# Own tiles for queries and keys, loads issued in four places of a batch, tail scores one batch ahead: attention with a routed expert layer behind it

## The chip, the cores and the metric

The kernel runs on one core of a Trainium2 chip. The metric is the device time of one execution in microseconds (us), taken as the median of several executions.

## The reference, cut to what matters

Eight batches of eight heads of retention attention (a causal product without a softmax, each head with its own decay), and then a mixture of eight experts of which each token takes one:

```python
# q, k, v: (8, 8, 576, 64); x: 4608 tokens of 512; w1: (8, 512, 1024); w2: (8, 1024, 512)
scores = scale * np.matmul(q, k.transpose(0, 1, 3, 2))
Dmat = np.where(rel >= 0, gamma[:, None, None] ** rel[None, :, :], 0.0)
ret = scores * Dmat[None, :, :, :]
attn_out = np.matmul(ret, v)
...
expert_idx = np.argmax(logits, axis=1)
h = np.maximum(x[mask] @ w1[e], 0.0)
out[mask] = gate_w[mask, None] * (h @ w2[e])
```

## The kernel before, in words

**Two stages.** The attention runs batch by batch over roughly the first quarter of the time; the experts follow. Within a manual schedule every engine, and the queue of SyncE (SP) on which nearly all transfers are issued, does its work in the order in which the program writes it. So a transfer that waits for its buffer holds up the transfers written behind it.

**One batch.** A batch has 576 positions: four chunks of 128 and a tail of 64. Heads go in pairs p = 0 to 3. `load_qk(b, p)` (L525) brings queries and keys of one pair into one tile `qkt` of two halves, by one transfer (two for batch 0); the pool has eight such tiles, two batches' worth. `load_k` (L537) brings the keys a second time in the other layout (`kt`, two buffers), `load_v` (L544) the values (`vt`, two buffers). `load_batch(b)` (L940) issues all six in a row: four `qkt`, then `kt`, then `vt`.

**The loop** (L1036) runs, for each batch b from 1, `scores(b)`, `tokens(b - 1)`, `products(b)`, and then `load_batch(b + 2)`:

- `scores(b)` (L979): for each pair `emit_A` (L710), the products of keys and queries inside the chunks (L716, TensorE), which VectorE multiplies by the decay (L725); behind each, `scale_q` (L704) on GpSimd. At its end `scale_k(b + 1)` (L683, GpSimd) on the next batch's `kt`.
- `tokens(b - 1)` (L989): the router's work for the batch before: logits (L905, L913), ranks, transposes of four or five tiles of tokens (L882) that ScalarE copies into `y` (L883) and SP stores to `xd` (L886).
- `products(b)` (L1005): `emit_U` (L733, L743: keys times values), `emit_O` (L791, L799: scores times values), `emit_At` (L831, L838: the scores of the tail, then the decay on VectorE into `pt`, L840), `emit_S` (L807, L815: the state times the queries) and `emit_Ot` (L845, L855: the tail's output, from `pt`).

`qkt` of batch b is read last by `emit_Ot(b)`, `kt` of batch b by `emit_U(b)`, `vt` of batch b by `emit_Ot(b)`; the loads of batch b + 2 take these buffers.

**PSUM banks.** There are eight. `Banks.tile` (L110) hands them out: in batch 0 from two rings of four, from batch 1 on from one ring of eight (`Banks.joint`, set at L1039), and behind the loop from a list of free banks (`Banks.loose`, L121), to which `done` (L125) returns one when the program has written its last use. Which buffer a matmul has to wait for follows from this order alone.

**Behind the loop** (L1047 on) come the last routing and the first expert's products, in an order written out by hand.

Of the kernel before, what the change touches and what calls it, by code (L numbers as in the profile page):

```python
# [95 lines left out]
def retention_moe(ctx: ExitStack, tc: tile.TileContext, qk, kn, v0s, vs, w1, w2, head, cst, out):  # L96
# [28 lines left out]
    def done(ps):  # L125

        if Banks.loose is not None:
            Banks.loose.append(ps)
# [375 lines left out]
    with ExitStack() as att:  # L504
# [2 lines left out]
        a2 = att.enter_context(tc.tile_pool(name="a2", bufs=2))  # L507
        a1 = att.enter_context(tc.tile_pool(name="a1", bufs=1))

        qkt, xT, xC = {}, {}, {}  # L510
        w0 = {}

        def w0_load(c):
# [8 lines left out]

        both = (nc.sync, nc.scalar)

        def load_qk(b, p):  # L525
            t = qkp.tile([P, 2, S], F32, name="qkt")
            if b == 0:
                for i, on in enumerate(both):
                    on.dma_start(out=t[:, i], in_=qk[b, p, i])
            else:  # L530
                nc.sync.dma_start(out=t, in_=qk[b, p].rearrange("i p s -> p i s"))
            qkt[b, p] = t

        kt, vt_ = {}, {}
        KW = NCH * DM
# [155 lines left out]
        def turn_k(p):  # L691

            ps = psa.tile([P, 512], F32, name="a")
            for c in range(NCH):
                nc.tensor.transpose(ps[:, c * P : (c + 1) * P], qkt[0, p][:, 1, c * P : (c + 1) * P], ident)
            g = cc("gneg").rearrange("p (c h) -> p c h", c=NCH)[:, :, 2 * p : 2 * p + 2]
            nc.vector.tensor_tensor(
                out=kview(0)[:, :, p * P : (p + 1) * P].rearrange("p c (h d) -> p c h d", h=2),
                in0=ps.rearrange("p (c h d) -> p c h d", c=NCH, h=2),
                in1=g.unsqueeze(3).broadcast_to([P, NCH, 2, D]),  # L700
                op=ALU.mult,
            )

        def scale_q(b, p):  # L704
            q = qkt[b, p][:, 0, P : NCH * P]
            nc.gpsimd.tensor_tensor(out=q, in0=q, in1=gsb[:, p, :], op=ALU.mult)  # L706

        Pm, Pt = {}, {}

        def emit_A(b, p):  # L710
            t = qkt[b, p]
            ps = [psa.tile([P, 512], F32, name="a") for _ in range(2)]
            for c in range(NCH):
                for h in range(2):
                    hs = slice(h * D, (h + 1) * D)
                    nc.tensor.matmul(  # L716
                        ps[h][:, c * P : (c + 1) * P],
                        t[hs, 1, c * P : (c + 1) * P],
                        t[hs, 0, c * P : (c + 1) * P],
                        start=True,  # L720
                        stop=True,
                    )
            pm = raws[(0, 1, 4, 5)[p]][:, :1024].rearrange("p (h c n) -> p h c n", h=2, c=NCH)
            for h in range(2):
                nc.vector.tensor_tensor(  # L725
                    out=pm[:, h],
                    in0=ps[h].rearrange("p (c n) -> p c n", c=NCH),
                    in1=decay[:, 2 * p + h].unsqueeze(1).broadcast_to([P, NCH, P]),
                    op=ALU.mult,
                )  # L730
            Pm[b, p] = pm

        def emit_U(b):  # L733
            k, v, T = kview(b), vview(b), Tst
            for c2 in range(NCH // 2):
                ps = psm.tile([P, 512], F32, name="m")
                u = ps.rearrange("p (c r d) -> p c r d", c=2, r=NP)
                for ci in range(2):
                    c = 2 * c2 + ci
                    for p in range(NP):  # L740
                        for h in range(2):
                            hd = 2 * p + h
                            nc.tensor.matmul(  # L743
                                u[h * D : (h + 1) * D, ci, p, :],
                                k[:, c, hd * D : (hd + 1) * D],
                                v[:, c, hd, :],
                                start=True,
                                stop=True,
                            )
                for ci in range(2):  # L750
                    c = 2 * c2 + ci
                    if c == 0:
                        nc.scalar.copy(T[:, 0], u[:, 0])
                    else:
                        nc.vector.tensor_tensor(out=T[:, c], in0=u[:, ci], in1=T[:, c - 1], op=ALU.add)

        def emit_U0(g):
            k, v, T = kview(0), vview(0), Tst
# [48 lines left out]
        def emit_S(b, g):  # L807

            T = Tst
            x, xc = x_tiles(b)  # L810
            for c in range(1, NCH):
                for p in (2 * g, 2 * g + 1):
                    for h in range(2):
                        hs = slice(h * D, (h + 1) * D)
                        nc.tensor.matmul(  # L815
                            Po[b, p][side(p, h), c * P : (c + 1) * P],
                            T[hs, c - 1, p, :],
                            qkt[b, p][hs, 0, c * P : (c + 1) * P],
                            start=False,
                            stop=(c == NCH - 1),  # L820
                        )
            for p in (2 * g, 2 * g + 1):
                po = Po.pop((b, p))
                if b % 2 == 0:
                    nc.scalar.copy(x[:, p, :], po)
                else:
                    copy = nc.vector.tensor_copy if (b, g) == (B - 1, 1) else nc.scalar.copy
                    copy(xc[:, p, D:], po[:, :D])
                    copy(x[:, p, : 512 - D], po[:, D:])

        def emit_At(b):  # L831
            ps = psa.tile([P, 512], F32, name="a")
            u = ps[:, : NP * TL].rearrange("p (r n) -> p r n", r=NP)
            for p in range(NP):
                for h in range(2):
                    hs = slice(h * D, (h + 1) * D)
                    t = qkt[b, p]
                    nc.tensor.matmul(u[hs, p, :], t[hs, 1, 512:], t[hs, 0, 512:], start=True, stop=True)  # L838
            pt = a2.tile([P, NP, TL], F32, name="pt")
            nc.vector.tensor_tensor(  # L840
                out=pt, in0=u, in1=cc("decayt").rearrange("p (r n) -> p r n", r=NP), op=ALU.mult
            )
            Pt[b] = pt

        def emit_Ot(b):  # L845
            vt, T, pt = vtview(b), Tst, Pt.pop(b)
            ps = [(psm if b else psa).tile([P, 512], F32, name="m") for _ in range(2)]
            u = [x[:, : NP // 2 * TL].rearrange("p (r n) -> p r n", r=NP // 2) for x in ps]
            for r in range(NP // 2):
                for last in (False, True):  # L850
                    for odd in range(2):
                        p = 2 * r + odd
                        for h in range(2):
                            hs = slice(h * D, (h + 1) * D)
                            nc.tensor.matmul(  # L855
                                u[odd][side(p, h), r, :],
                                T[hs, NCH - 1, p, :] if last else vt[hs, p, :],
                                qkt[b, p][hs, 0, 512:] if last else pt[hs, p, :],
                                start=(r == 0 and not last),
                                stop=(r == NP // 2 - 1 and last),  # L860
                            )
            x, xc = x_tiles(b)
            dst = xc[:, :, :TL] if b % 2 == 0 else x[:, :, 512 - D :]
            g = cc("gtail").rearrange("p (r n) -> p r n", r=NP)
            for odd in range(2):
                nc.vector.tensor_tensor(out=dst[:, odd::2], in0=u[odd], in1=g[:, odd::2], op=ALU.mult)


        def tile_src(b, g):
# [109 lines left out]
        def scores(b):  # L979
            for p in range(NP):  # L980
                emit_A(b, p)
                scale_q(b, p)
                if (b, p) == (B - 1, 0):
                    for i in range(3):
                        gather(0, i, BEG)
            if b + 1 < B:
                scale_k(b + 1)

        def tokens(b):  # L989
# [6 lines left out]
                route_onehot(b - 1)  # L996
            for g in range(group_tiles(b)[1]):
                route_tile(b, g)
            route_turn(b)
            if b == B - 2:  # L1000
                for i in range(2):
# [3 lines left out]
        def products(b):  # L1005
            end = b == B - 1
            emit_U(b)
            if end:
                xprep(0, 2)
                w0_load(2)  # L1010
# [7 lines left out]
            if end:  # L1018
                low = [w0_high(0), w0_high(1, nc.gpsimd)]
                w0_load(3)  # L1020
            emit_At(b)
            if end:
                for split in low:
                    split()
# [11 lines left out]
        for b in range(B):  # L1036
            if b == 0:
                first_batch()
                Banks.joint = every  # L1039
            else:  # L1040
                scores(b)
                tokens(b - 1)
                products(b)
            if b + 2 < B:
                load_batch(b + 2)
        loose_banks()
        b = B - 1  # L1047
        gates_power(slice(0, NT - 5))
        first = [mm1_in(PAIRS[0], 0)]
# [554 lines left out]
```

## Time and profile before

| what | value |
|---|---|
| median of 3 runs | 570.35 us (569.89 to 570.95) |
| the profiled execution's own time | 571.25 us |
| its span, first to last instruction | 569.3 us |
| mean granted TensorE clock | 1.000 |
| TensorE (PE) busy | 98% of the span |
| VectorE (DVE) / ScalarE (ACT) / GpSimd (POOL) busy | 73% / 67% / 42% |

In the rows PE is TensorE's matmul, PEld its weight load, and a name with q is the queue of that engine. L716 is line 716. A row of a group of instructions gives the busy time and the mean of one; a row of waits gives us in total, how many, and the longest. "issue" is time in which an engine waited for nothing that the profile shows. DMA share is the mean busy share of the 16 DMA engines.

### The profile page before, as it was taken

How to read it: one execution, taken by the hardware profiler on the slowest of the kernel's cores; microseconds unless marked ns; L12 is line 12 of the kernel's file. 1: busy time of each engine (PE TensorE's matmuls, PEld its weight loads, DVE VectorE, ACT ScalarE, POOL GpSimd, SP SyncE). 2: the span in 40 equal slices, each digit the busy share in tenths (PEclk: the TensorE clock that was granted, in tenths of full speed). 3: DMA queues.
4: the chain of work that ended last, by engine and by line, in shares of the span. 5: the costliest groups of instructions: out<-in, count | busy, mean ns of one | idle time of the engine just before them, and what ended most of it. 6: DMA issues, size and time to landing. Idle time of an engine off the chain costs nothing.

```text
span 569.3 us, 13412 instructions
## 1 busy us (share of the span) xinstructions
PE 556.9 (98%) x5258; PEld 510.1 (90%) x5258; DVE 417.3 (73%) x938; ACT 381.7 (67%) x696; POOL 236.6 (42%) x233
## 2 busy tenths in 40 slices
PE   9999998999999999999999999999999999999996
PEld 8888898999998899889989988998899899889986
DVE  4755778779876868877887888688778778786810
ACT  1246554447759887987787788779877877867611
POOL 6674345554456740562065126405620750242012
PEclk9999999999999999999999999999999999999999
DMA  9999999877469583557447445837574574422201
GB/s 319 390 395 340 350 335 378 307 269 266 167 207 184 174 201 119 148 161 185 122 145 206 129 117 186 186 111 168 163 150 131 156 200 133 133 101 84 75 38 49
DMA packets 81089, 109.24 MB, mean 192 GB/s; under 512 B 42328, under 2 KB 43772, under 8 KB 81024
## 3 DMA queue, kind: packets, MB, share of 16 engines
q1 hardware_dynamic: 71920, 86.24, 50.0%
q0 software_dynamic: 7696, 19.95, 10.7%
q10 hardware_dynamic: 1408, 2.17, 1.1%
q8 instruction: 42, 0.69, 0.5%
q14 instruction: 23, 0.19, 0.1%
HBM read 80.27 MB, written 19.94 MB: 176 GB/s over the span
## 4 chain that ended last, share of the span: by engine, by line
PE 78%; DMA 12%; issue 3%; DVE 3%; ACT 2%; POOL 1%; POOLq 0%; SPq 0%; ACTq 0%; DVEq 0%
PE m L1281 19%; PE a L1213 15%; PE m L1213 11%; PE a L1281 10%; DMA out<-y,sid 9%; PE a L716 3%; PE a L459 2%; PE a L799 2%; PE m L716 2%; PE m L459 2%; DMA xd<-y 2%; PE m L799 2%; PE a L882 1%; PE m L882 1%; PE m L743 1%
## 5 line engine op out<-in xcount | busy, mean ns | idle before, releaser
L1281 PE MATMUL m<-w2s,hs 128*128 128x512 f32 x600 | 138.8, 389 | 0.0
L1281 PEld LDWEIGHTS m<-w2s,hs 128*128 128x128 f32 x600 | 112.3, 188 | 22.9
L1257 POOL DMA_INDIRECT out<-y,sid x41 | 47.0, 1147 | 193.0 <-DVE wsum L1135 125.7
L1281 PE MATMUL a<-w2s,hs 128*128 128x512 f32 (+1 forms) x384 | 83.6, 376 | 0.0
L1281 PEld LDWEIGHTS a<-w2s,hs 128*128 128x128 f32 x384 | 68.9, 188 | 13.1
L1213 PE MATMUL a<-xsb,w0s 128*128 128x320 f32 x342 | 57.9, 309 | 0.0
L375 POOL DMA_INDIRECT gt<-gd,gid x40 | 44.7, 1118 | 18.4 <-issue 10.8
L1213 PEld LDWEIGHTS a<-xsb,w0s 128*128 128x128 f32 x342 | 52.1, 188 | 0.0
L1184 ACT ACTIVATE hs<-y 128x320 fp32r<-128x320 f32 x84 | 39.3, 474 | 17.8 <-DVE y L1225 16.7
L362 POOL DMA_INDIRECT raw<-xd,gid x40 | 42.7, 1069 | 19.3 <-DVE sid L352 7.6
L1177 DVE SCALAR_TENSOR_TENSOR hs<-y,hs 128x320 fp32r<-128x320 f32 x84 | 46.6, 568 | 2.0
L687 POOL TENSOR_TENSOR kt<-kt,cs 128x512 f32<-128x512 f32 x28 | 28.4, 1045 | 46.1 <-DMA kt<-kn 46.1
L410 ACT COPY raw<-raw 128x1024 uint16<-128x1024 uint16 x35 | 47.5, 1356 | 0.0
L445 ACT CAST xsb<-raw 128x128 fp32r<-128x128 f32 x70 | 32.1, 459 | 21.6 <-DVE raw L428 20.9
L1112 DVE TENSOR_TENSOR w2s<-raw,w2s 128x1024 fp32r<-128x1024 f32 x32 | 39.1, 1222 | 6.7 <-ACT w2s L1109 6.6
L1225 DVE TENSOR_TENSOR y<-a,y 128x320 f32<-128x320 f32 x47 | 22.7, 486 | 20.3 <-ACT y L1229 14.0
L403 ACT COPY raw<-raw 128x1024 uint16<-128x1024 uint16 x35 | 35.4, 1045 | 0.0
L1109 ACT CAST w2s<-raw 128x1024 fp32r<-128x1024 f32 x32 | 33.4, 1045 | 2.4 <-DMA raw<-w 2.4
L706 POOL TENSOR_TENSOR qkt<-qkt,gsb 128x384 f32<-128x384 f32 x32 | 31.3, 1006 | 7.2 <-DMA xd<-y 2.9
L1213 PE MATMUL m<-xsb,w0s 128*128 128x320 f32 x198 | 34.0, 309 | 0.0
L421 DVE TENSOR_TENSOR raw<-raw 128x256 f32<-128x256 f32 x35 | 14.8, 424 | 26.1 <-ACT raw L410 26.1
L1225 DVE TENSOR_TENSOR y<-m,y 128x320 f32<-128x320 f32 x37 | 18.1, 488 | 18.7 <-ACT y L1229 13.2
(258 smaller groups left out, 1198.5 us busy)
## 6 DMA issues: line engine op xcount, KB each, us to landing
raw<-w SPq DMA_DIRECT2D x64, 512.0 KB, 3.9
qkt<-qk SPq DMA_DIRECT2D x28, 576.0 KB, 7.9
xd<-y SPq DMA_DIRECT2D x36, 256.0 KB, 9.9
vt<-vs SPq DMA_DIRECT2D x7, 1152.0 KB, 13.1
kt<-kn SPq DMA_DIRECT2D x7, 1024.0 KB, 10.9
qkt<-qk ACTq DMA_DIRECT2D x4, 288.0 KB, 5.3
qkt<-qk SPq DMA_DIRECT2D x4, 288.0 KB, 5.4
out<-y,sid POOLq DMA_INDIRECT x41, 3.3
```

The source lines that it names most:

```text
L362: nc.gpsimd.indirect_dma_start(out=t[:, XO : XO + DM], out_offset=None, in_=xd[:rows, :], in_offset=bass.IndirectOffsetOnAxis(ap=gid[:, a ...
L375: nc.gpsimd.indirect_dma_start(out=g[:, i : i + 1], out_offset=None, in_=gd[:, :], in_offset=bass.IndirectOffsetOnAxis(ap=gid[:, a : a + 1 ...
L403: nc.scalar.copy(far.rearrange("p (h n) -> p h n", h=2), near.rearrange("p (n h) -> p h n", h=2))
L410: nc.scalar.copy(far.bitcast(U16).rearrange("p (n h) -> p h n", h=2), near.rearrange("p (h n) -> p h n", h=2))
L1109: nc.scalar.copy(hi, u)
L1112: nc.vector.tensor_tensor(out=lo, in0=u, in1=hi.bitcast(F32), op=ALU.subtract)
L1177: nc.vector.scalar_tensor_tensor(out=lo, in0=part(src), scalar=0.0, in1=hi.bitcast(F32), op0=ALU.max, op1=ALU.subtract)
L1184: nc.scalar.activation(hi, part(src), AF.Relu)
L1213: nc.tensor.matmul(ps[:, :HC], w[:, ws, ka, d * P : (d + 1) * P], xop(kx, xsp)[:, d, :], start=(n in (1, 2, 5) and d == 0 and k == 0), sto ...
L1225: nc.vector.tensor_tensor(out=out[:, :HC], in0=x[:, :HC], in1=out[:, :HC], op=ALU.add)
L1257: put = nc.gpsimd.indirect_dma_start(out=out.rearrange("t (k n) -> (t k) n", k=k), out_offset=bass.IndirectOffsetOnAxis(ap=rows, axis=0), ...
L1281: nc.tensor.matmul(ps[:, :step], hs[:, hsp, f, i * P : (i + 1) * P], w[:, ws, f, n : n + step], start=(j == 0 and k == 0), stop=(j == NF - ...
```

## The change

Queries and keys get a tile each, of half the size, so that the keys' buffer of batch b is free of queries. The loads of a later batch are issued in four places instead of one: the keys of pair p of batch b + 2 behind `emit_A(b, p)`, the values of batch b + 1 behind the token tiles of `tokens(b - 1)`, `kt` of batch b + 2 behind `emit_U(b)`, and the queries of batch b + 2 at the end, where all of them were. The tail's scores are computed one batch ahead: `products(b)` calls `emit_At(b + 1)` where it called `emit_At(b)`, batch 1's are computed at the end of its `scores`, and the last batch's `products` has none. Banks come from the free list from batch 1 on.

```diff
+        def load_q(b, p):
+            qt[b, p] = qkp.tile([P, S], F32, name="qt")
+            nc.sync.dma_start(out=qt[b, p], in_=qk[b, p, 0])
+
+        def load_kT(b, p, on=nc.sync):
+            kT[b, p] = qkp.tile([P, S], F32, name="kT")
+            on.dma_start(out=kT[b, p], in_=qk[b, p, 1])
+
         def load_qk(b, p):
-            t = qkp.tile([P, 2, S], F32, name="qkt")
-            if b == 0:
-                for i, on in enumerate(both):
-                    on.dma_start(out=t[:, i], in_=qk[b, p, i])
-            else:
-                nc.sync.dma_start(out=t, in_=qk[b, p].rearrange("i p s -> p i s"))
-            qkt[b, p] = t
+            load_q(b, p)
+            load_kT(b, p, nc.sync if b else nc.scalar)
...
         def emit_A(b, p):
-            t = qkt[b, p]
+            q, k = qt[b, p], kT[b, p]
...
+                done(ps[h])
...
         def scores(b):
             for p in range(NP):
                 emit_A(b, p)
+                if 0 < b < B - 2:
+                    load_kT(b + 2, p)
                 scale_q(b, p)
...
+            if b == 1:
+                emit_At(b)
             if b + 1 < B:
                 scale_k(b + 1)
...
             for g in range(group_tiles(b)[1]):
                 route_tile(b, g)
+            if b + 2 < B:
+                load_v(b + 2)
             route_turn(b)
...
             emit_U(b)
+            if b + 2 < B:
+                load_k(b + 2)
...
-            emit_At(b)
+            if not end:
+                emit_At(b + 1)
...
             if b == 0:
                 first_batch()
-                Banks.joint = every
+                loose_banks()
+                for p in range(NP):
+                    load_kT(b + 2, p)
+                load_k(b + 2)
             else:
                 scores(b)
                 tokens(b - 1)
                 products(b)
             if b + 2 < B:
-                load_batch(b + 2)
-        loose_banks()
+                for p in range(NP):
+                    load_q(b + 2, p)
         b = B - 1
```

The other hunks put `done(...)` behind the last use of each bank in `emit_U`, `emit_S`, `emit_At` and `emit_Ot`, and write `qt` or `kT` where `qkt` stood.

## Rows read from the trace of the kernel before

**Rows 1.** The page, part 1: TensorE's busy time and instructions.

```profile
PE 556.9 (98%) x5258; PEld 510.1 (90%) x5258; DVE 417.3 (73%) x938; ACT 381.7 (67%) x696; POOL 236.6 (42%) x233
```

**Rows 2.** Busy time by stretch: span, PE, PEld, DVE, ACT, POOL, clock, DMA share, GB/s.

```profile
20.00:40.00 20.00, 19.24 (x439) 18.04 (x440) 11.48 (x31) 8.87 (x24) 12.02 (x13) 1.00 1.05 390
80.00:100.00 20.00, 18.22 (x434) 17.25 (x434) 14.16 (x40) 10.87 (x28) 7.94 (x8) 1.00 1.04 381
160.00:180.00 20.00, 20.00 (x141) 18.89 (x141) 12.41 (x28) 14.56 (x26) 9.77 (x10) 1.00 0.93 210
```

**Rows 3.** TensorE's waits in the first 200 us: total us, times, longest.

```profile
PE a L716 <- DMA xd<-y: 1.8, 1, 1.8
PE m L855 <- issue: 1.5, 1, 1.5
...
PE m L595 <- PEq L1595: 0.7, 1, 0.7
...
PE a L799 <- issue: 0.2, 1, 0.2
```

**Rows 4.** TensorE's timeline, 15 to 150 us: start, us, instruction, idle before it.

```profile
21.19 0.49 PE L716 MATMUL a<-qkt 64*128 64x128 f32 x4
...
40.89 1.29 PE L716 MATMUL m<-qkt 64*128 64x128 f32 x18 [1.15 <-issue]
...
89.95 0.37 PE L716 MATMUL a<-qkt 64*128 64x128 f32 x1 [1.78 <-DMA xd<-y]
...
122.82 2.06 PE L716 MATMUL a<-qkt 64*128 64x128 f32 x32
```

**Rows 5.** Busy time and counts from 0 to five of the waits' starts, columns as above.

```profile
0.00:39.74 39.74, 38.49 (x727) 35.74 (x728) 23.33 (x67) 11.76 (x29) 26.57 (x37) 1.00 1.01 365
0.00:53.08 53.08, 50.69 (x981) 47.02 (x981) 31.29 (x90) 18.72 (x47) 33.73 (x45) 1.00 1.02 372
...
0.00:70.19 70.19, 66.97 (x1361) 62.22 (x1362) 43.55 (x123) 27.02 (x68) 39.87 (x51) 1.00 0.99 358
0.00:88.10 88.10, 83.37 (x1742) 77.72 (x1742) 57.04 (x156) 36.30 (x92) 49.32 (x60) 1.00 0.99 356
...
0.00:120.39 120.39, 113.38 (x2375) 105.88 (x2376) 80.29 (x227) 51.94 (x132) 63.76 (x75) 1.00 0.98 353
```

**Rows 6.** The page, part 3, the queue that carries instructions: packets, MB, share.

```profile
q8 instruction: 42, 0.69, 0.5%
```

**Rows 7.** Queues from 87.40 to 87.60 us.

```profile
q8 instruction: 1, 0.02, 31.9%
```

**Rows 8.** Queues from 89.95 to 94.55 us (no other queue has a row).

```profile
q1 hardware_dynamic: 756, 1.64, 101.1%
```

**Rows 9.** Queues from 89.95 to 94.70 us: the row that is new.

```profile
q8 instruction: 1, 0.02, 1.3%
```

**Rows 10.** Queues from 103.36 to 104.65 us.

```profile
q1 hardware_dynamic: 241, 0.43, 88.1%
q8 instruction: 1, 0.02, 6.1%
```

**Rows 11.** The page, part 6: transfers, count, KB each, median us to landing.

```profile
qkt<-qk SPq DMA_DIRECT2D x28, 576.0 KB, 7.9
xd<-y SPq DMA_DIRECT2D x36, 256.0 KB, 9.9
vt<-vs SPq DMA_DIRECT2D x7, 1152.0 KB, 13.1
kt<-kn SPq DMA_DIRECT2D x7, 1024.0 KB, 10.9
```

**Rows 12.** Busy time in four stretches of 4 us, columns as in the stretches above.

```profile
52.00:56.00 4.00, 3.38 (x106) 3.08 (x104) 2.73 (x9) 2.15 (x4) 2.04 (x3) 1.00 0.70 261
56.00:60.00 4.00, 4.00 (x93) 3.68 (x90) 3.84 (x7) 0.11 (x1) 3.69 (x4) 1.00 0.82 243
72.00:76.00 4.00, 4.00 (x84) 3.81 (x77) 3.99 (x9) 0.00 (x0) 3.43 (x4) 1.00 0.84 243
104.00:108.00 4.00, 4.00 (x121) 3.93 (x115) 3.60 (x11) 2.31 (x8) 2.70 (x3) 1.00 0.56 128
```

**Rows 13.** GpSimd's timeline: the keys' scaling waits for its load.

```profile
24.15 4.05 POOL L687 TENSOR_TENSOR kt<-kt,cs 128x512 f32<-128x512 f32 x4 [4.90 <-DMA kt<-kn]
...
35.89 4.08 POOL L687 TENSOR_TENSOR kt<-kt,cs 128x512 f32<-128x512 f32 x4 [3.83 <-DMA kt<-kn]
```

**Rows 14.** The chain that ended last: the tail's scores of batch 1.

```profile
34.33 0.61 PE m L838 x16
```

**Rows 15.** The queue of SP: issue of four loads, start and us.

```profile
36.69 3.18 SPq L531 DMA_DIRECT2D qkt<-qk  x4
```

More of the change, by code (lines that the diff above doesn't have):

```diff
@@ L508, in retention_moe @@
         a1 = att.enter_context(tc.tile_pool(name="a1", bufs=1))
-        qkt, xT, xC = {}, {}, {}
+        qt, kT, xT, xC = {}, {}, {}, {}
         w0 = {}
@@ L694, in turn_k @@
             for c in range(NCH):
-                nc.tensor.transpose(ps[:, c * P : (c + 1) * P], qkt[0, p][:, 1, c * P : (c + 1) * P], ident)
+                nc.tensor.transpose(ps[:, c * P : (c + 1) * P], kT[0, p][:, c * P : (c + 1) * P], ident)
             g = cc("gneg").rearrange("p (c h) -> p c h", c=NCH)[:, :, 2 * p : 2 * p + 2]
@@ L704, in scale_q @@
         def scale_q(b, p):
-            q = qkt[b, p][:, 0, P : NCH * P]
+            q = qt[b, p][:, P : NCH * P]
             nc.gpsimd.tensor_tensor(out=q, in0=q, in1=gsb[:, p, :], op=ALU.mult)
@@ L717, in emit_A @@
                         ps[h][:, c * P : (c + 1) * P],
-                        t[hs, 1, c * P : (c + 1) * P],
-                        t[hs, 0, c * P : (c + 1) * P],
+                        k[hs, c * P : (c + 1) * P],
+                        q[hs, c * P : (c + 1) * P],
                         start=True,
@@ L755, in emit_U @@
                         nc.vector.tensor_tensor(out=T[:, c], in0=u[:, ci], in1=T[:, c - 1], op=ALU.add)
+                done(ps)
         def emit_U0(g):
@@ L817, in emit_S @@
                             T[hs, c - 1, p, :],
-                            qkt[b, p][hs, 0, c * P : (c + 1) * P],
+                            qt[b, p][hs, c * P : (c + 1) * P],
                             start=False,
@@ L829, in emit_S @@
                     copy(x[:, p, : 512 - D], po[:, D:])
+                done(po)
         def emit_At(b):
@@ L836, in emit_At @@
                     hs = slice(h * D, (h + 1) * D)
-                    t = qkt[b, p]
-                    nc.tensor.matmul(u[hs, p, :], t[hs, 1, 512:], t[hs, 0, 512:], start=True, stop=True)
+                    nc.tensor.matmul(u[hs, p, :], kT[b, p][hs, 512:], qt[b, p][hs, 512:], start=True, stop=True)
             pt = a2.tile([P, NP, TL], F32, name="pt")
@@ L843, in emit_At @@
             Pt[b] = pt
+            done(ps)
         def emit_Ot(b):
@@ L857, in emit_Ot @@
                                 T[hs, NCH - 1, p, :] if last else vt[hs, p, :],
-                                qkt[b, p][hs, 0, 512:] if last else pt[hs, p, :],
+                                qt[b, p][hs, 512:] if last else pt[hs, p, :],
                                 start=(r == 0 and not last),
@@ L866, in emit_Ot @@
                 nc.vector.tensor_tensor(out=dst[:, odd::2], in0=u[odd], in1=g[:, odd::2], op=ALU.mult)
+                done(ps[odd])
         def tile_src(b, g):
```

## The prediction

> **What bounds the kernel now.** I began with the page's busy times: TensorE is busy 98% of the span [rows 1]. A load order can only win where it waits, so I went on to the busy time by stretch. There the experts' stage has no gap (20.00 of 20 us), while the attention loses 0.8 us of 20 at its start and 1.8 us at 80 to 100, and in those stretches the DMA engines are full, at 381 to 390 GB/s [rows 2]. TensorE's waits of the first 200 us come to eight lines, 7.4 us together, of which 0.7 are the start [rows 3]. So some 6.7 us, 1.2% of the time, is all that the waits shown could give back.
>
> None of these waits names a tile that the instruction reads or writes: most say "issue", and the longest is put down to a store of tokens. I counted what TensorE had done when they came. Matmuls and weight loads together stand at 1455, 1962, 2723, 3484 and 4751 [rows 5]; the differences are 507, 761, 761 and 1267, that is 2, 3, 3 and 5 times 253.5. The queue named "instruction" moved 42 packets of 16 KB [rows 6], and 10,516 matmuls and weight loads [rows 1] over 42 make 250 each. So TensorE waits at the ends of blocks of its own program. The wait before 89.95 us shows the course: a block came between 87.40 and 87.60 [rows 7], TensorE went on at 89.95 [rows 4], some 2.4 us behind it. The next packet came only 4.60 to 4.75 us later, with the load queue at 101% of 16 engines [rows 8, 9]. At 103.36, where that queue was running dry, it came within 1.3 us [rows 10]. So a block takes 4.65 + 2.4 = 7.0 us behind a full queue and 1.3 + 2.4 = 3.7 behind an empty one. A batch takes (122.82 - 21.19) / 6 = 16.9 us from batch 1 to 7 [rows 4], and a block (120.39 - 39.74) x 253.5 / (4751 - 1455) = 6.2 us [rows 5]. A full load queue therefore makes TensorE late, an empty one doesn't.
>
> The Trainium skill, "Runtime: NRT & Kernel Launch", section "Instruction fetch mechanics", says that instructions come in 16 KiB blocks of 256 and that the cost of crossing a boundary is "mostly hidden". By that rule the waits would have another cause and the change would leave them all. The block size agrees with the trace; "hidden" does not, behind a full queue.
>
> **The change part by part.** The sum is made against the profiled execution: 571.25 us, a span of 569.3 and 1.95 around it. That is 0.90 above the median of 570.35.
>
> *Bytes.* Nothing is saved: a batch loads 4 x 576 + 1152 + 1024 = 4480 KB and stores 4.5 x 256 KB [rows 11], 5.77 MB. At 388 GB/s that is 14.9 us of the 16.9 that a batch lasts. However the loads are spread, the queue has work for 88% of the time; spreading decides when, and how much lies in it.
>
> *When.* Keys (1.18 MB) are issued some 14 us earlier than now, `kt` (1.05 MB) some 7 us earlier, queries as now, values some 8 us later. On the whole the queue is given work earlier. The idle of the DMA engines, 30% of 52 to 56, 18% of 56 to 60 and 16% of 72 to 76 us [rows 12], 2.5 us together, gets filled; the other lull at 104 to 108 (44%) gets longer and starts sooner. So the first four batches have a full queue throughout, and the refills there stay as late as they are. What is won is won in batches 5 and 6: 2.5 us x 388 GB/s, nearly 1 MB, less in the queue. The waits that I find there are 1.78 us at 89.95 [rows 4], and about 0.5 each at 103 and 120, among the lines left out between the first and the last of the waits [rows 3]. I take half of these 2.8 us: **-1.4**. Ends: nothing (another block is late instead), and all 6.7 us of the waits shown if every block comes in time.
>
> *Tail scores one batch ahead.* This needs queries and keys of batch 2 while batch 1 is in its products. `kt` of batch 1 landed at 24.15 [rows 13]. Behind it on the queue now lie values of batch 1 (1.18 MB), then keys, `kt` and queries of batch 2 (1.18 + 1.05 + 1.18): 4.59 MB, 11.8 us, so the queries land at 36.0. The same sum for the old order (1.18 + 2.36 + 1.05) gives 36.0 for `kt` of batch 2; it landed at 35.89 [rows 13]. TensorE comes to these scores at 34.33, plus 0.5 for batch 1's that are now in front: 34.8 [rows 14]. It waits **+1.2 us**, and the state's and tail's products queue behind it. Further on it closes: values of batch 2 land at 36.0 + 3.41 MB / 388 = 44.8, some 1 us before they are needed, queries of batch 3 at 50.5, some 2 before. Ends: 0, if the refill that is late in this place anyway covers it, and 3 us, if the next two come late as well. The scores' own 0.6 us moves from batch 7 to batch 1: nothing.
>
> *Queue of SP.* Four more transfers a batch. Four cost 3.18 us of issue in a full queue [rows 15], of 16.9; nothing is issued late by it, since SP waits for buffers most of the time. Each new place stands behind work that TensorE has done by then. Cost 0; if SP were held up, the stores would be late, which only the routing reads.
>
> *Banks.* No wait of TensorE names a reader of a bank [rows 3]; a list in the order of release, with at most four banks of `emit_O` out, takes the place of a ring. Nothing, at most 0.5 us either way, by the shorter gaps behind the copies at a batch's end. `done` issues no instruction.
>
> *GpSimd and VectorE.* `kt` lands earlier, so GpSimd waits less than the 4.9 and 3.8 us of [rows 13]; TensorE isn't behind it, so nothing. The decay on the tail's scores has the same place on VectorE, and leaves batch 7: between 0 and -0.4.
>
> Sum: -1.4 + 1.2 - 0.2 = -0.4, 570.85 for the profiled execution, and 0.90 less for the median: **569.9 us**. That is no change: what a measurement here can tell is 0.2%, 1.14 us.
>
> **Rivals.**
>
> *The refills come in time (faster).* If a refill's wait goes by how much lies in the queue just then, and not by whether it has work, shorter bursts of at most some 2 MB, where 4.6 MB were issued at once, let most blocks of batches 3 to 7 through. Then the waits from 60 us on go (1.5, 1.8, 0.5, 0.5 and 0.2, 4.5 us), less 1.2 for the first: 570.35 - 3.3 = 567.0. For it: 1.3 us against 4.65 [rows 8 to 10]. Against it: 88% of the time has work to move. At its far end all 6.7 go and blocks that now come just in time gain too, down to 563. Half-size transfers for queries and keys would help the same way. The Trainium skill, "DMA: Bandwidth & Descriptors", section "Queues, rings and completion order", says that a DMA engine goes round its queues packet by packet; by that rule smaller transfers put less in front of a refill. No row here separates transfer sizes.
>
> *Data late in the first batches (slower).* The order puts keys that are needed 25 us later ahead of values and queries needed within 15. If the queries of batch 2 land 1 us later than my sum, at 37, the wait is 2.2; everything behind shifts little, as the queue is full, so the wait stays. If blocks 2 to 4 are late besides, by 0.5 each, no gain later: 570.35 + 3.0 = 573.3. It decides from the point where the queue at 24 us holds over 4.6 MB in front of these queries.
>
> *The waits have another cause, or stay as they are.* Only the 1.2 remain: 571.5; the smaller part of slower.
>
> **How the numbers follow.** Forecast, within 0.2% of the median: 0.38, since the bytes and their rate don't move and the two terms nearly cancel. Refills in time: 0.37, of which 0.07 are below 565.5. Slower: 0.25, two thirds of it at 571.5 to 573 and 0.07 beyond. The range leaves out 0.07 below and 0.07 to 0.1 above: 565.5 to 572.8. The likeliest case alone spans 569.2 to 571.5.
>
> **What would show it.** TensorE's timeline: a wait of about 1 us at L838 near 34 to 36 us, put down to a load of queries. DMA share at 1.0 without a dip from 20 to about 90 us, and low by 110. Refill waits again at multiples of 253.5 instructions, as many as before up to 90 us and fewer behind. Batch 7's first scores at 122 to 123 us. I am wrong if they stand before 121.5 or after 124, or if TensorE waits for a bank or for values.

## The result, and the profile after

The changed kernel takes 573.49 us (median of 6 runs, 572.54 to 574.39) against 570.12 us for the kernel before in the same rounds (6 runs, 569.63 to 570.95): 1.0057 times the time, 95% interval 1.0042 to 1.0071. In later rounds the ratio was 1.0043 (1.0022 to 1.0063). The change makes the kernel slower by about half a percent; no change was forecast, and the time lies above the range.

The profiled execution took 574.04 us, its span is 572.2 us, 2.9 us longer than before. TensorE's busy time has hardly moved. The page of the changed kernel, part 1:

```profile
PE 557.0 (97%) x5258; PEld 509.8 (89%) x5258; DVE 420.8 (74%) x938; ACT 381.5 (67%) x696; POOL 239.4 (42%) x233
```

The same work stands as in [rows 1], but VectorE is busy 3.5 us longer and GpSimd 2.8 us longer with the same number of instructions. So time was added as waiting on TensorE, and as longer instructions on those two. (GpSimd's say little: they are 240.2 us in the run with `kt` late, below, which has no loss.) TensorE's waits of the first 200 us, changed kernel, in the form of [rows 3]:

```profile
PE a L719 <- issue: 4.2, 3, 1.7
PE m L861 <- issue: 1.3, 1, 1.3
PE m L843 <- DMA qt<-qk: 0.8, 2, 0.4
PE a L747 <- DVE tab L333: 0.8, 1, 0.8
PE m L598 <- PEq L1614: 0.8, 1, 0.8
PE a L804 <- DVE tab L333: 0.6, 1, 0.6
PE m L912 <- issue: 0.6, 1, 0.6
PE m L258 <- DVE oh L200: 0.4, 1, 0.4
PE a L459 <- DVE w0s L521: 0.4, 1, 0.4
PE a L719 <- DMA qt<-qk: 0.3, 1, 0.3
PE m L747 <- issue: 0.3, 1, 0.3
PE m L394 <- DMA raw<-xd,gid: 0.2, 1, 0.2
```

Without the start (0.8) they come to 9.9 us, where before there were 6.7. By cause:

| what TensorE waits for | before | after |
|---|---|---|
| blocks of its own program ("issue", and the wait put down to a store) | 6.7 | 4.2 + 1.3 + 0.6 + 0.3 = 6.4 |
| queries still on the queue | none listed | 0.8 (batch 2) + 0.3 (batch 0) = 1.1 |
| VectorE (DVE) | none listed | 0.8 + 0.6 ("tab") + 0.4 ("oh") + 0.4 ("w0s") = 2.2 |
| a gather | none listed | 0.2 |

The difference, 3.2 us, is what the span grew by, to 0.3 us. But this is the account of one execution. A second profile of the changed kernel, from the later rounds (span 570.5 us), has

```profile
PE a L719 <- issue: 3.1, 2, 1.9
PE a L747 <- DVE tab L333: 1.3, 2, 0.8
PE m L843 <- DMA qt<-qk: 0.8, 2, 0.4
...
PE a L804 <- DVE tab L333: 0.6, 1, 0.6
```

and 3.9 us of "issue" in all, where the first profile has 6.4. So the waits for batch 2's queries and on "tab" come back, and those at block ends differ by 2.5 us between two executions of one kernel.

The large "issue" waits are still at block ends: the counts up to three of them, changed kernel, columns as in [rows 5],

```profile
0.00:41.30 41.30, 37.70 (x725) 35.05 (x726) 22.91 (x67) 11.76 (x29) 27.77 (x38) 1.00 1.00 365
0.00:60.30 60.30, 55.08 (x1106) 51.51 (x1107) 36.66 (x103) 20.61 (x50) 38.10 (x48) 1.00 1.02 372
0.00:90.40 90.40, 83.05 (x1740) 77.66 (x1741) 59.02 (x160) 37.25 (x93) 51.10 (x61) 1.00 1.02 374
```

are 1451, 2213 and 3481, which are 762 and 1268 apart, 3 and 5 blocks of 253.5. The queue now works with hardly a break up to 112 us, and then rests. Five stretches of the changed kernel, the first three also in [rows 12]:

```profile
52.00:56.00 4.00, 4.00 (x128) 3.76 (x124) 1.90 (x9) 2.31 (x6) 0.00 (x0) 1.00 1.04 375
72.00:76.00 4.00, 4.00 (x104) 3.93 (x96) 3.07 (x10) 2.04 (x7) 1.93 (x3) 1.00 1.06 394
104.00:108.00 4.00, 3.95 (x122) 3.62 (x119) 1.86 (x10) 2.21 (x8) 0.00 (x0) 1.00 1.04 386
112.00:116.00 4.00, 4.00 (x76) 3.63 (x70) 3.90 (x8) 2.51 (x6) 4.00 (x6) 1.00 0.24 88
124.00:128.00 4.00, 4.00 (x112) 3.93 (x106) 3.04 (x11) 2.05 (x4) 1.29 (x2) 1.00 0.02 4
```

TensorE's timeline of the changed kernel shows the waits for queries, batch 0's first and then batch 2's, and the start of batch 7:

```profile
5.55 1.16 PE L719 MATMUL a<-qt,kT 64*128 64x128 f32 x16 [0.31 <-DMA qt<-qk]
...
34.98 0.33 PE L843 MATMUL m<-qt,kT 64*64 64x64 f32 x4 [0.42 <-DMA qt<-qk]
...
125.21 1.16 PE L719 MATMUL m<-qt,kT 64*128 64x128 f32 x16
```

Batch 7 begins at 125.21, where it began at 122.82 [rows 4]; the other 0.5 us of the 2.9 are lost behind it.

**VectorE.** The waits on "tab" and "oh" name operations of the router. Those on "tab" come at 100.8 and 117.7 us, in batches 5 and 6; those on "w0s" and "oh" come at 142.6 and 149.9 us, behind the batches. L747 and L804 don't read `tab`: what ties them to L333 is a PSUM bank that L333 has still to read. In batch 6 VectorE's timeline of the changed kernel reads:

```profile
112.93 0.68 DVE L728 TENSOR_TENSOR raw<-a,decay 128x512 f32<-128x512 f32 x1
113.53 0.18 DVE L266 TENSOR_TENSOR t<-m,oh 128x32 f32<-128x32 f32 x1
113.74 0.19 DVE L272 TENSOR_REDUCE tok_all<-t 128x4 f32<-128x32 f32 x1
113.96 1.08 DVE L275 SCALAR_TENSOR_TENSOR si<-tok_all 128x4 int32<-128x4 f32 x1
115.08 0.97 DVE L279 TENSOR_SCALAR ai<-si 128x4 int32<-128x4 int32 x1
115.96 1.09 DVE L280 TENSOR_SCALAR ai<-si 128x4 int32<-128x4 int32 x1
116.97 0.19 DVE L282 TENSOR_REDUCE s<-oh 128x8 f32<-128x32 bf16 x1
```

and in the kernel before, the same three operations:

```profile
112.16 0.17 DVE L275 SCALAR_TENSOR_TENSOR si<-tok_all 128x4 int32<-128x4 f32 x1
112.36 0.17 DVE L279 TENSOR_SCALAR ai<-si 128x4 int32<-128x4 int32 x1
112.43 0.17 DVE L280 TENSOR_SCALAR ai<-si 128x4 int32<-128x4 int32 x1
```

Operations on four numbers per partition take six times as long. What runs beside them is GpSimd's scaling of `kt`, four pieces in 4.06 us. In the changed kernel:

```profile
112.97 4.06 POOL L690 TENSOR_TENSOR kt<-kt,cs 128x512 f32<-128x512 f32 x4
```

In the kernel before it waited for its load until these operations were done:

```profile
119.06 4.05 POOL L687 TENSOR_TENSOR kt<-kt,cs 128x512 f32<-128x512 f32 x4 [8.09 <-DMA kt<-kn]
```

So the early load of `kt` took away a wait of GpSimd (46 us in seven batches, 8 us now), and that wait had kept GpSimd off these operations. The two engines met in the kernel before too, but elsewhere. The router's choice of expert for a later step, from 20 to 152 us (count, us in total, mean ns), before:

```profile
L196 DVE SCALAR_TENSOR_TENSOR w<-L_all,wme 128x32 f32<-128x32 f32 (+1 forms) x8 | 5.4, 678 | 0.3
L200 DVE TENSOR_TENSOR oh<-wm,wme 128x32 bf16<-128x32 f32 (+1 forms) x8 | 3.8, 470 | 0.3
```

and after:

```profile
L196 DVE SCALAR_TENSOR_TENSOR w<-L_all,wme 128x32 f32<-128x32 f32 (+1 forms) x8 | 1.6, 196 | 0.3
```

L200 has 1.6 us, too, after. TensorE's waits before name none of these [rows 3]. The change did not make the two engines meet; it moved their meeting onto operations that TensorE waits for.

### The profile page after: what moved, and what is told of

The parts are those of the page before. It is cut to its first block, busy times and chain, and to the rows that moved or that the text cites. A ratio compares the mean times of both kernels' runs of the same rounds, so it can differ in the third digit from the quotient of the medians.

```text
span 572.2 us, 13468 instructions
## 1 busy us (share of the span) xinstructions
PE 557.0 (97%) x5258; PEld 509.8 (89%) x5258; DVE 420.8 (74%) x938; ACT 381.5 (67%) x696; POOL 239.4 (42%) x233
## 4 chain that ended last, share of the span: by engine, by line
PE 73%; DMA 13%; issue 5%; DVE 4%; POOL 2%; ACT 2%; POOLq 0%; SPq 0%; DVEq 0%; ACTq 0%
PE a L1300 15%; PE m L1300 13%; PE m L1232 13%; PE a L1232 13%; DMA out<-y,sid 9%; PE a L719 3%; PE m L459 3%; PE a L804 2%; DMA qt<-qk 2%; PE a L459 1%; PE m L719 1%; PE m L804 1%; PE a L820 1%; DMA raw<-w 1%; DVE raw L728 1%
## 5 line engine op out<-in xcount | busy, mean ns | idle before, releaser
L1300 PE MATMUL a<-w2s,hs 128*128 128x512 f32 (+1 forms) x528 | 119.6, 385 | 0.0
L1300 PEld LDWEIGHTS a<-w2s,hs 128*128 128x128 f32 x528 | 97.3, 188 | 19.3
L1300 PE MATMUL m<-w2s,hs 128*128 128x512 f32 (+1 forms) x456 | 103.0, 384 | 0.0
L1300 PEld LDWEIGHTS m<-w2s,hs 128*128 128x128 f32 x456 | 83.9, 188 | 16.7
L709 POOL TENSOR_TENSOR qt<-qt,gsb 128x384 f32<-128x384 f32 x32 | 31.5, 1007 | 46.7 <-PE m L719 32.7
L1232 PE MATMUL m<-xsb,w0s 128*128 128x320 f32 x276 | 46.3, 309 | 0.0
L1232 PE MATMUL a<-xsb,w0s 128*128 128x320 f32 x264 | 44.6, 309 | 0.0
L1232 PEld LDWEIGHTS m<-xsb,w0s 128*128 128x128 f32 x276 | 41.9, 188 | 0.0
L1244 DVE TENSOR_TENSOR y<-m,y 128x320 f32<-128x320 f32 x49 | 23.8, 488 | 24.7 <-ACT y L1248 17.5
L1232 PEld LDWEIGHTS a<-xsb,w0s 128*128 128x128 f32 x264 | 40.2, 188 | 0.0
```

What stands on the lines that cost most here:

```text
L1232: nc.tensor.matmul(ps[:, :HC], w[:, ws, ka, d * P : (d + 1) * P], xop(kx, xsp)[:, d, :], start=(n in (1, 2, 5) and d == 0 and k == 0), sto ...
L1300: nc.tensor.matmul(ps[:, :step], hs[:, hsp, f, i * P : (i + 1) * P], w[:, ws, f, n : n + step], start=(j == 0 and k == 0), stop=(j == NF - ...
```

## The experiments

All ratios are to the kernel before, in the same rounds. Single executions on these chips spread over some 5 us, so an interval is about 0.2% (1.1 us) either way.

**kt late again.** The changed kernel with one part undone.

```diff
@@ products(b)
-            if b + 2 < B:
-                load_k(b + 2)
@@ loop, behind the four load_q(b + 2, p)
+                if b:
+                    load_k(b + 2)
```

> The changed kernel with kt of batch b + 2 loaded at the batch's end again, behind the queries (batch 0 as in the change). Theory (GpSimd's scaling of kt, started some 7 us earlier because kt lands earlier, now runs beside VectorE's rank operations and stretches them from 0.17 to about 1 us, so TensorE waits for VectorE): the scaling moves back behind the products, the waits on DVE tab (0.8 + 0.6 us) go, 571.5 us, 2 below the changed kernel. Rival (it is only the queue: late queries of batch 2 and late refills): the same bytes, no more than 0.5 us below, 573.

Measured: 570.65 us, 0.9997 (0.9973 to 1.0021). The theory holds: with `kt` late the loss is gone within the interval, and the waits on "tab" are gone from TensorE's list. The waits on "oh" and "w0s" are still in it (0.5 and 0.4 us), so they are not what the loss is made of. This run moves a load as well; the next one does not.

**GpSimd held back.** The loads stay; the scaling starts behind the state sums.

```diff
@@ scores(b): scale_k(b + 1) taken out
@@ products(b), behind load_k(b + 2)
+            if b + 1 < B:
+                nc.gpsimd.tensor_copy(pin, Tst[:, NCH - 1, 0, :1])
+                scale_k(b + 1)
```

> The changed kernel with all loads where it has them, but GpSimd's scaling of kt for the next batch held back behind the sums of the states (a one-column copy from their last tile in front of it on GpSimd, in the products). Theory (clash of GpSimd and VectorE): rank operations back to 0.17 us, no wait on DVE tab, 571.3 us. Rival (queue and refills alone): the loads are unchanged, so 573.5.

Measured: 571.30 us, 1.0013 (0.9993 to 1.0033). In batch 6 GpSimd now runs behind the same operations,

```profile
117.69 0.18 POOL L1024 COPY pin<-Tst 128x1 f32<-128x1 f32 x1 [5.94 <-DVE bump L242]
117.82 4.04 POOL L692 TENSOR_TENSOR kt<-kt,cs 128x512 f32<-128x512 f32 x4
```

and these are back to their length, while the router's next steps (L341, L344) have become long:

```profile
112.78 0.16 DVE L275 SCALAR_TENSOR_TENSOR si<-tok_all 128x4 int32<-128x4 f32 x1
112.97 0.17 DVE L279 TENSOR_SCALAR ai<-si 128x4 int32<-128x4 int32 x1
113.05 0.17 DVE L280 TENSOR_SCALAR ai<-si 128x4 int32<-128x4 int32 x1
...
118.06 0.83 DVE L341 TENSOR_SCALAR t<-tab 128x3 f32<-128x3 f32 x1
118.92 0.96 DVE L344 SCALAR_TENSOR_TENSOR t<-t,tab 128x3 f32<-128x3 f32 x1
```

TensorE's list has no wait on "tab" any more. Nothing about the loads was changed here, so it is GpSimd's time that counts, not the queue. How much of the loss goes is less sure: the interval meets the changed kernel's second one (1.0022 to 1.0063).

**kt early in the kernel before.**

```diff
@@ load_batch(b)
-            load_k(b)
+            if b < 3:
+                load_k(b)
@@ products(b), behind emit_U(b)
+            if b + 2 < B:
+                load_k(b + 2)
```

> The kernel before with one part of the change alone: kt of batch b + 2 loaded behind the products of keys and values instead of at the batch's end. Theory (clash): rank operations stretch and TensorE waits for VectorE, 572 us, about 2 above before. Rival (queue and refills): 570 or slightly less, since 1 MB is moved out of the burst at the batch's end.

Measured: 572.42 us, 1.0029 (1.0010 to 1.0049). This one part makes the kernel before slower, by the same route; of TensorE's waits here:

```profile
PE m L743 <- DVE tab L333: 0.9, 1, 0.9
...
PE m L799 <- DVE tab L333: 0.6, 1, 0.6
PE a L799 <- DVE tab L331: 0.6, 1, 0.6
```

**Queries first for batch 2.** In the changed kernel, `load_k(2)` stands behind the four `load_q(2, p)`.

> The changed kernel with the queries of batch 2 ahead of kt of batch 2 on the queue (1.05 MB less in front of them, 2.7 us). Theory: the 1.1 us that TensorE waits for queries at batch 2's tail scores goes, 572.4 us. Rival (the refill that is due in the same place would be late anyway and takes the wait's place): 573.5, with a wait named issue near 36 us instead.

Measured: 572.89 us, 1.0030 (1.0011 to 1.0049). The wait for queries is gone from TensorE's list and batch 2 begins some 1.5 us sooner; of this, 0.2 us go to the block that is late at 40 us (1.96 where the changed kernel waited 1.74). In the trace the theory holds, for the 0.8 us that are batch 2's (the other 0.3 of its 1.1 us belong to batch 0), and the rival has a small part. In time it is not shown: the interval meets both of the changed kernel's.

**The last batch's tail scores in the last batch.**

```diff
-            if not end:
+            if b + 1 < B - 1:
                 emit_At(b + 1)
+            if end:
+                emit_At(b)
```

> The changed kernel with the last batch's tail scores in the last batch again (the others stay a batch ahead). Theory: in the last batch TensorE waits for VectorE anyway, so its 0.45 us there are free, and in batch 6 they are on the path: 573.0 us, 0.4 below the changed kernel, the waits on DVE w0s and DVE oh behind 140 us gone. Rival: it makes no difference where the 0.45 us stand, 573.4.

Measured: 572.41 us, 1.0031 (1.0010 to 1.0051): lower than the changed kernel's 1.0057 and 1.0043, but the intervals overlap. In its profile the wait on "oh" is still there (0.4 us), that on "w0s" is 0.2. Not settled by this run.

**The tail scores alone**, a batch ahead in the kernel before, loads untouched.

> The kernel before with the tail's scores a batch ahead, as in the change, and its loads as they were (queries and keys of batch 2 still ahead of kt). Theory: no wait for queries near 35 us, but 0.45 us of TensorE move from the last batch, where VectorE sets the pace, to batch 1: 1.0007 of before. Rival (the place of these scores costs nothing): 1.000; (they cost more than the late queries did): 1.002.

Measured: 571.07 us, 1.0006 (0.9991 to 1.0020). At most 0.2%; theory and rival are not told apart.

**Banks.** First the changed kernel with the ring, then the kernel before with the list, then the changed kernel beside the latter.

> The changed kernel with the ring of eight banks for batches 1 to 7 instead of the free list. Theory (the banks were at no time what TensorE waited for, other than through VectorE being late): 573.4 us, as the changed kernel. Rival (the list hands out a bank that is released later than the ring's would be): 572 or less, with the waits on DVE tab gone.

> The kernel before with the list of free banks in place of the ring from batch 1 on, and nothing else of the change. Theory (no wait of TensorE names a bank): 1.000 of before, at most 0.1% either way. Rival (the list has a part in the 0.57%, as the ring's 1.0035 may suggest): 1.002.

> The changed kernel unchanged, on the chip and in the rounds of the two runs above: 1.0057 of before, 1.0042 to 1.0071. If it is near 1.0035 here, the kernel with the ring was no different from it.

Measured: 573.54 us, 1.0035 (1.0016 to 1.0054) with the ring; 571.10 us, 1.0006 (0.9991 to 1.0021) for the list alone; 573.36 us, 1.0043 (1.0022 to 1.0063) for the changed kernel again. With the ring the waits on "tab" stay (0.9 and 0.6 us). The list has no share that can be seen, and none over 0.2%.

**All costs taken back, twice.** Once with `kt` at the batch's end behind the queries, once with the loads spread and GpSimd held back; both with queries first and the last tail scores in the last batch.

> The changed kernel with three things taken back: kt loaded at the batch's end behind the queries (for batch 2 too), and the last batch's tail scores computed in the last batch. Theory (the three costs add up): 573.4 less 2 for the clash, 1.1 for the late queries, 0.4 for tail scores that batch 7 had free: 569.9 us, level with before. Rival (one cost hides another): 571 or more.

> The changed kernel with its loads where it has them (but queries of batch 2 ahead of kt of batch 2), the scaling of kt held back on GpSimd as in the gate experiment, and the last batch's tail scores in the last batch: the spread of the loads without its three costs. Theory (the spread by itself moves no fewer bytes and gives nothing): 570 us, level with before. Rival (spread loads let the blocks through, the gain was only hidden): 567 to 568.

Measured: 571.00 us, 1.0006 (0.9981 to 1.0031), and 571.40 us, 1.0004 (0.9983 to 1.0025). Both are level with the kernel before. (The first is at 571.00 us, where its rival had it, but the kernel before took 570.66 in these rounds.) So what was taken back holds the loss, and `kt` alone is enough for it within the interval, as the first run shows; the tiles, the list and the other tail scores, which both still have, cost nothing that can be seen. Spreading the loads, without its costs, gives nothing: 567 to 568 lies outside the interval.

**Is it the full queue that makes blocks late?** Fewer bytes, in the kernel before:

```diff
         def load_v(b):
+            if b > 1:
+                vt_[b] = vt_[b - 2]
+                return
```

> The kernel before without the loads of the values of batches 2 to 7: these batches use the values of the batch two before, still in the buffer, so what is computed from them differs, and every instruction of the engines stays. 1.18 of 5.77 MB per batch are gone, so the queue has work for 12 of 17 us. Theory (blocks of TensorE's program come late behind a full load queue): the waits at block ends shrink from 6.7 to about 2 us, the last batch's scores begin at 117 to 119 us instead of 122.8, 566 us. Rival (the waits belong to the block ends whatever the queue does): 570, waits unchanged.

Measured: 567.52 us, 0.9926 (0.9899 to 0.9952). From 20 to 100 us the queue moves 311 GB/s at a share of 0.88, where the kernel before has 363 at 1.00; TensorE's waits without the start sum to 3.7 us instead of 6.7, and batch 7 begins at 119.80. The stretch and the batch's start in the kernel with fewer bytes:

```profile
20.00:100.00 80.00, 77.59 (x1715) 72.31 (x1712) 57.34 (x149) 39.85 (x102) 40.15 (x41) 1.00 0.88 311
```

```profile
119.80 2.06 PE L719 MATMUL a<-qkt 64*128 64x128 f32 x32
```

The time falls with the load on the queue, though less than expected (566). So do the waits (2 us were expected), but by 3 us, little more than the two profiles of the changed kernel differ by.

**Length of the pieces.** In the kernel before, by another arrangement of the arrays in memory: half as long, then values and `kt` twice as long; then the latter on the kernel with all costs taken back.

```diff
-NVS = 4
+NVS = 8        # 2 for the long pieces
-    kn = ...reshape(B - 1, P, NCH, DM)...
+    kn = ...reshape(B - 1, P, 2 * NCH, DM // 2)...
```

> The kernel before with the same transfers in pieces of half the length: runs of 1152 bytes (queries, keys, values) and 1024 bytes (kt) instead of 2304 and 2048, by another arrangement of the arrays in memory. Theory (a block of TensorE's program waits behind a fixed number of pieces that the engine of the queue has already taken up): the wait of a block behind a full queue falls from about 4 us to under 3, most of the 6.7 us of waits at block ends goes, 566 us. Rival (it waits for a time or for bytes, or shorter pieces lower the rate): the waits stay or grow, 570 to 574.

> The kernel before with values and kt in pieces of twice the length (4608 and 4096 bytes), queries and keys as they were. Theory (fixed number of pieces): blocks behind values and kt come some 2 us later, TensorE waits more, 575 to 580 us. Rival (time or bytes): 570.

> The changed kernel with the three things taken back (kt at the batch's end behind the queries, the last batch's tail scores in the last batch), and values and kt in pieces of 4608 and 4096 bytes. Theory (full-queue time decides: the longer pieces move 400 GB/s instead of 390 and free the queue 2 to 3% sooner): 568.5 to 569.5 us, below before. Rival (the rate is not what decides): 570.5, as without the longer pieces.

Measured: 574.83 us, 1.0070 (1.0045 to 1.0095) with short pieces; 571.59 us, 1.0011 (0.9990 to 1.0031) with long ones; 570.14 us, 0.9966 (0.9941 to 0.9991) with long ones on the repaired kernel. Both theories of a fixed number of pieces failed: a block does not wait behind a fixed number of them. From 20 to 100 us the short pieces move

```profile
20.00:100.00 80.00, 72.87 (x1615) 67.92 (x1613) 54.98 (x143) 36.77 (x93) 39.56 (x40) 1.00 1.07 356
```

356 GB/s at a share of 1.07, where the kernel before has 363 at 1.00, and the waits at block ends come to 8.1 us. That the lower rate is what costs the time is argued, not shown: long pieces in the kernel before moved 370 GB/s in this stretch, and gave nothing. The repaired kernel, first without long pieces and then with them, has

```profile
20.00:100.00 80.00, 75.48 (x1699) 70.87 (x1697) 53.24 (x149) 39.39 (x101) 41.55 (x42) 1.00 1.03 375
```

```profile
20.00:100.00 80.00, 77.08 (x1715) 72.20 (x1715) 53.33 (x148) 39.93 (x102) 43.45 (x44) 1.00 1.02 381
```

So long pieces add 6 GB/s and 16 matmuls in the same 80 us. The ratio is 0.34% below before, with an interval that ends just short of no change; by the medians (570.14 against 571.08) it is 0.2%. That it is faster than the changed kernel is clear; that it is faster than the kernel before hangs on this margin, so the theory is not settled by it.

## Why the prediction was wrong

**What bounds the kernel: right.** TensorE waits at the ends of blocks of its program while the load queue is full. The counts after, and the run with fewer bytes, bear it out.

**Bytes and "When": right about the first lulls, wrong about the next one; the gain is open.** The share stayed at 1.0 where it had dipped at 52 to 60 and at 72 to 76 us, as forecast. The lull at 104 to 108 us was to start sooner; that stretch is full now (1.04), and the lull comes at 112. So batches 5 and 6, where the gain was sought, still had a busy queue in front of their blocks (shares of 0.87 to 1.04 in the 4 us stretches from 92 to 112 us). The blocks at 103 and 120 us come in time now, but others at 60, 78 and 108 us do not. The refills gave back 0.3 us in one profile (6.7 to 6.4) and 2.8 in the other (3.9), on either side of the 1.4 forecast. That spreading the bytes gives nothing in time is what the repaired kernel with spread loads shows, 1.0004 (0.9983 to 1.0025).

**Tail scores one batch ahead: right, at two thirds of the size.** 1.2 us of waiting were forecast near 35 us; 0.42 and 0.42 at L843 were found, by the late queries of batch 2, and the last of them was there by 35.73, where the forecast had 36.0.

**"GpSimd and VectorE": the step that failed.** It said that GpSimd waits less, and "TensorE isn't behind it, so nothing". GpSimd was costed as if only those who wait for its results could feel it. Its scaling moved some six us ahead, onto those of the router's small operations on VectorE that stand in front of the sum into `tab`; they went from 0.17 to about 1 us each, and TensorE waited 1.4 us (1.9 in the second profile) for that sum to free a bank. Three runs show it: `kt` late takes the whole loss away, holding GpSimd back takes most of it by the middle of the intervals, and `kt` early alone gives 1.0029 to the kernel before. All runs agree: where `kt` is early and GpSimd free, in the change and in four other kernels, TensorE waits 1.4 to 2.5 us on "tab" and the ratio is 1.0029 to 1.0057; in the four kernels with `kt` late or GpSimd held and the pieces as they were, that wait is not in the list and the ratio is 0.9997 to 1.0013. The other 0.8 us of waiting for VectorE is no part of this. The wait on "tab" is not the whole of the loss, which is 3.4 us by the first medians and 2.5 by the later ones; how the rest divides between the queries and the block ends is not shown.

The rule that bears on it was there to be used: the Trainium skill, "SBUF — State Buffer", section "Who interferes with whom", says that a VectorE instruction with two SBUF inputs contends with a GpSimd one that reads SBUF, that one in a two-port mode contends with GpSimd, whoever issues first holding the shared ports for the whole instruction, and that on trn2 `tensor_reduce` never contends. The trace agrees: 1.08, 0.97 and 1.09 us are the length of one piece of GpSimd's (4.06 / 4 = 1.02), and the reductions at L272 and L282 kept their 0.19. L275 has two inputs in SBUF; that L279 and L280, with one, run in a two-port mode is shown by no row.

**"The scores' own 0.6 us moves: nothing", banks: nothing.** For the list this is shown, within 0.2%. Yet TensorE did wait for a bank, which the prediction named as a sign of being wrong: VectorE was late in reading it, with the ring as with the list. For the scores a cost of up to 0.2% is not excluded; that the last batch had these 0.45 us free, because VectorE sets the pace there, was argued and not shown.

**The rivals.** The slower one named late data as its mechanism; this part came smaller than the forecast itself had it, and the cost that turned the sign was in none of them. That its 573.3 us lies beside the measured 573.49 is luck. Batch 7's first scores stand at 125.21 us, past the 124 that the prediction gave as a sign of being wrong. By the sum, -1.4 + 1.2 - 0.2 became, in the first profile, -0.3 at block ends, 0.8 for batch 2's queries, 1.4 on "tab", 0.8 on "oh" and "w0s", and 0.3 and 0.2 for batch 0's queries and a gather: 3.2 us. In the second profile the waits come to 7.4 us, only 0.7 more than before, because the block ends give 2.8 back; the 1.4 to 1.9 us on "tab" and the 0.8 for queries are in both. No run shows the -0.2 by itself.

## What to carry to other kernels

Before a load is made earlier, look at which engine has been waiting for it and what will run beside that engine's work at the new time: a wait off the critical path can be what decides at which operations two engines meet. Where TensorE waits with no releaser, count its instructions up to there; equal steps mean that its own program arrives late. Here fewer bytes on the queue helped (0.9926), and the order of the loads did not (1.0004). When data is asked for earlier by one batch, walk the queue in order of issue for the first batches, where the backlog is deepest.

## What the runs showed of the hardware that was not expected

VectorE operations on four numbers took 0.97 to 1.09 us instead of 0.17 beside GpSimd's multiplications in SBUF, while VectorE's multiplications that read PSUM kept 0.68 us beside the same engine. Pieces of half the length cost the queue 2% of the rate that the kernel before reached (356 against 363 GB/s, at a share of 1.07 against 1.00), and the kernel took 1.0070 of the time. Two executions of one kernel waited 6.4 and 3.9 us at the ends of its program's blocks.
